# Infini-attention with a GEGLU gate: one broadcast tile for all head groups, the residual loaded once per segment, guard squares in halves

## The chip, the core and the metric

The kernel runs on one core of one Trainium2 chip. A core has five engines that run side by side, each with a queue of its own that is worked off in order: PE (matrix products; PEld is its loading of weights), DVE and POOL (elementwise work), ACT (functions by table), SP (here: it starts DMA transfers). DMAs are started by an instruction on an engine's queue and land later; engines wait for one another, and for DMAs, by semaphores. An instruction that waits holds up everything behind it in its queue. Times are device microseconds (us) of one execution; the figure given for a kernel is the median of its runs.

## What is computed

`x` has 2048 rows of 448; there are 16 heads of 28. The result is `x + attn * silu(gelu(xn wg) * (xn wu) wd)` with `xn` the layer norm of `x`.

```python
for s in range(4):                       # segments of 512 rows
    p = softmax(qs @ ks^T * 28**-0.5, causal within the segment)
    a_dot = p @ vs
    a_mem = (phi(qs) @ M) / (phi(qs) @ z + 1e-6)     # phi(t) = t+1 if t>0 else exp(t)
    o = g * a_mem + (1 - g) * a_dot                  # g = sigmoid(beta), one per head
    M += phi(ks)^T @ vs ;  z += sum(phi(ks))
s = o @ wo
out = x + s * silu((gelu(xn @ w_gate) * (xn @ w_up)) @ w_down)
```

## The kernel before

All of it is in `fast_path`. The rows are taken in 4 segments `s` of 512, each as 4 blocks of 128. The heads are padded from 28 to 32 and lie in 4 groups of 4, so that a group fills 128 partitions; the spare columns of a head make the denominators.

The program's order is written by hand (L523 to L581): the layer norm and the projections of segment 0; then for each segment `gate_up(s)`, 14 steps of 8 products each (gate, then up, then GELU on ACT and a product on DVE into `hT`), and `attention(s)`, 24 slots (4 groups x 3 banks x 2 head pairs). `gate_up(3)` comes after `attention(3)`, and after it the down projection and the finish of each block. Between steps and slots stand other pieces, by a table of step numbers (`in_turn`) or, in attention, as fill by weight. `tick` counts steps, slots and fill units; `later(n, fn)` issues `fn` n ticks on.

One slot of attention: `scores` puts K^T Q of two heads on PE (L337), ACT takes the exponential into `pt` (L341), POOL sets the masked half of the diagonal block to zero (L344, one or two per slot). Two banks later `pv` multiplies by V on PE (L354) into the one `pv` buffer that there is, and after a group's last bank `evac` copies it out on DVE (L364) and sends the denominators, one row per head, to DRAM (`den`, L366). The last two banks of a segment (`ends`) are issued at the head of the next `gate_up` or attention.

The denominators: `invert` (L379) loads all 16x512 of a segment and side (softmax, or memory) spread on 128 partitions (`dc`, L383), and 3 ticks on DVE multiplies by the gate and inverts. Four DMAs on SP write four copies to DRAM (`rdr`, L390), and four more, one per group, read them back repeated 32 times per head (`rb`, one 128x512 tile per group, L393). POOL multiplies the memory result by its `rb` (`scale_memory`, L401), and the softmax result by its own, adding the two (`combine`, L410 and L411).

`finish_units`: for a block, SP loads 128 rows of `x` again (`xr`, L458), PE multiplies by `wo` (L461), DVE multiplies by the SiLU part (L464), POOL adds `xr` (`o_out`, L466), SP stores (L467). Blocks of segment s-1 are finished within attention s, those of segment 3 at the end.

`guard` squares the raw query and key weights on ACT (L157) at step 4 of `gate_up(0)` and sums them on PE at step 9, for a bound on the scores; the first tile that held the query weights is one of the two buffers `oT`.

SP's queue carries nearly all DMAs, in program order: `den`, `dc`, `rdr`, `rb`, `xr`, the stores. A store waits for POOL's `o_out`, and whatever stands behind it in the queue waits too.

Of the kernel before, what the change touches and what calls it, by code (L numbers as in the profile page):

```python
# [8 lines left out]
ACT = mybir.ActivationFunctionType  # L9
ALU = mybir.AluOpType  # L10
# [15 lines left out]
def fast_path(tc, A_x, A_wq, A_wk, A_wv, A_wo, A_beta, B_w_gate, B_w_up, B_w_down, out):  # L26
# [16 lines left out]
    with ExitStack() as ctx:  # L43
# [8 lines left out]
        oup = pool("oup", 4)  # L52
        rbp = pool("rbp", 4)
        blk = pool("blk", 5)
# [28 lines left out]
        wq_raw = seg2.tile([DC, NDC, D], BF16, name="oT")  # L83
        wk_raw = const.tile([DC, NDC, D], BF16, name="wk_raw")
        wv_sb = const.tile([DC, NDC, D], BF16, name="wv_sb")
# [55 lines left out]
        def later(n, fn):  # L141
            waiting.append((clock[0] + n, len(waiting), fn))

        def tick():
            clock[0] += 1
            due = sorted(w for w in waiting if w[0] <= clock[0])
            waiting[:] = [w for w in waiting if w[0] > clock[0]]
            for _, _, fn in due:
                fn()
# [3 lines left out]
        def guard():  # L153
            sqs = {}
            for i, nm in enumerate(("wq", "wk")):
                sqs[nm] = oup.tile([DC, NDC, D], BF16, name=f"oU{i}")
                nc.scalar.activation(out=sqs[nm][:], in_=raw[nm][:], func=ACT.Square)  # L157
            ones = const.tile([P, 1], BF16, name="ones")
            nc.gpsimd.memset(ones[:], 1.0)
            nrm = small.tile([1, 2, H], F32, name="nrm")  # L160
            yield
            for i, nm in enumerate(("wq", "wk")):
                np_ = ps_m.tile([P, L], F32, name="m")
                for c in range(NDC):
                    nc.tensor.matmul(out=np_[0:1, 0:D], lhsT=ones[0:DC, :], rhs=sqs[nm][:, c, :],
                                     start=(c == 0), stop=(c == NDC - 1))
                nc.vector.reduce_sum(out=nrm[:, i, :],
                                     in_=np_[0:1, 0:D].rearrange("p (h d) -> p h d", d=Dh), axis=AX.X)
            okh = small.tile([1, H], F32, name="okh")
            nc.vector.tensor_tensor(out=okh[:], in0=nrm[:, 0, :], in1=nrm[:, 1, :], op=ALU.mult)  # L170
            nc.vector.tensor_scalar(out=okh[:], in0=okh[:], scalar1=(LOGIT_MAX / (D * scale)) ** 2,
                                    scalar2=None, op0=ALU.is_lt)
            nc.vector.tensor_reduce(out=oki[:], in_=okh[:], op=ALU.min, axis=AX.X)
            yield
# [67 lines left out]
        def project_units(s):  # L242
# [37 lines left out]
            def ktok(b):  # L280
                kp = ps_m.tile([P, L], F32, name="m")
                for c in range(NDC):
                    nc.tensor.matmul(out=kp[:, 0:D], lhsT=xnT[s][:, c, b * P:(b + 1) * P],  # L283
                                     rhs=wk_raw[:, c, :], start=(c == 0), stop=(c == NDC - 1))
                e = work.tile([P, D], BF16, name="phk_e")
# [22 lines left out]
        def update(s):  # L308
# [10 lines left out]
            if s == 0:  # L319
                nc.vector.tensor_tensor(out=macc[:], in0=u[:], in1=bd, op=ALU.mult)  # L320
            else:
                um = rbp.tile([P, G, P], F32, name="rb")
                nc.vector.tensor_tensor(out=um[:], in0=u[:], in1=bd, op=ALU.mult)
                nc.gpsimd.tensor_tensor(out=macc[:], in0=macc[:], in1=um[:], op=ALU.add)
# [43 lines left out]
        def memory_read(s, g):  # L368
# [3 lines left out]
            if g == G - 1:  # L372
                later(2, lambda: invert(s, 1))
                for i in range(G):
                    later(11 + 2 * i, lambda i=i: scale_memory(s, i))

        rb = {}

        def invert(s, side):  # L379

            dc = small.tile([P, 64], F32, name="dc")
            rdr = dram.tile([H, 4, L], F32, name="rdr")
            nc.sync.dma_start(out=dc[:], in_=den[s][side].rearrange("h (c f) -> (h c) f", f=64))  # L383

            def rest():
                nc.vector.tensor_scalar(out=dc[:], in0=dc[:], scalar1=(1e-6 if side else 0.0),
                                        scalar2=igate[:, side:side + 1], op0=ALU.add, op1=ALU.mult)
                nc.vector.reciprocal(out=dc[:], in_=dc[:])
                for j in range(4):
                    nc.sync.dma_start(out=rdr[:, j, :].rearrange("h (c f) -> h c f", f=64), in_=dc[:])  # L390
                for g in range(G):
                    r = rbp.tile([P, L], F32, name="rb")
                    nc.sync.dma_start(  # L393
                        out=r[:], in_=rdr[g * HG:(g + 1) * HG].rearrange("h j l -> (h j) l")
                        .unsqueeze(1).to_broadcast([HG * 4, HP // 4, L]))
                    rb[s, g, side] = r
            later(3, rest)

        def scale_memory(s, g):
            o_n = oU[s, g, 1]  # L400
            nc.gpsimd.tensor_tensor(out=o_n[:], in0=o_n[:], in1=rb.pop((s, g, 1))[:], op=ALU.mult)  # L401

        def combine(s, g):
# [3 lines left out]
            if s == 0:  # L407
                nc.gpsimd.tensor_tensor(out=dst, in0=o_a[:], in1=r[:], op=ALU.mult)
            else:
                nc.gpsimd.tensor_tensor(out=o_a[:], in0=o_a[:], in1=r[:], op=ALU.mult)  # L410
                nc.gpsimd.tensor_tensor(out=dst, in0=o_a[:], in1=oU.pop((s, g, 1))[:], op=ALU.add)  # L411
# [19 lines left out]
        def down_units(s):  # L431
# [21 lines left out]
            return u  # L453

        def finish_units(s):
            def fin(b):
                xr = work.tile([P, D], BF16, name="xr")
                nc.sync.dma_start(out=xr[:], in_=x_v[s][:, b, :])  # L458
                a_ps = ps_m.tile([P, L], F32, name="m")
# [5 lines left out]
                o_out = work.tile([P, D], BF16, name="o_out")  # L465
                nc.gpsimd.tensor_tensor(out=o_out[:], in0=t[:], in1=xr[:], op=ALU.add)  # L466
                nc.sync.dma_start(out=o_v[s][:, b, :], in_=o_out[:])  # L467
            return [(0.75, lambda b=b: fin(b)) for b in range(NB)]
# [54 lines left out]
        with tc.manual_schedule():  # L523
# [4 lines left out]
            for s in range(NSEG):  # L528
                last = s == NSEG - 1

                if not last:
# [5 lines left out]
                    else:  # L537
                        in_turn(table, 4, [lambda: next(check)])
                        in_turn(table, 9, [lambda: next(check)])
                    layer_norm_steps(s + 1, table)  # L540
# [3 lines left out]
                if s + 2 < NSEG:  # L544
                    load_x(s + 2)
                if s == 2:
                    ok = nc.values_load(oki[0:1, 0:1], min_val=0, max_val=1)
                pre, lists, at = [], [], {}
                if last:
                    in_turn(at, 0, ends)  # L550
                    in_turn(at, 2, [lambda: invert(s - 1, 0)])
                    in_turn(at, 10, [lambda g=g: combine(s - 1, g) for g in range(G)])
                    in_turn(at, 15, [lambda g=g: memory_read(s, g) for g in range(G)])
                elif s > 0:
# [15 lines left out]

            s = NSEG - 1
            table = {}
            in_turn(table, 0, ends)
            in_turn(table, 2, [lambda: invert(s, 0)])
            in_turn(table, 9, [lambda g=g: combine(s, g) for g in range(G)])
            gate_up(s, table)
            dn, fi = down_units(s), finish_units(s)
            for b in range(NB):
                run(dn[3 * b:3 * b + 3])
                run(fi[b:b + 1])  # L580
        return ok  # L581

# [381 lines left out]
```

## Time and profile before

| | us |
|---|---|
| median of 3 runs (lowest to highest) | 333.48 (332.92 to 333.96) |
| the profiled execution | 333.42 |
| its span | 331.6 |
| PE busy in the span | 279.2 (84%) |
| DVE, ACT, POOL busy | 159.5, 152.0, 132.9 |
| mean granted PE clock, share of full speed | 0.951 |

The span is the time between the first and the last instruction in the trace; 1.8 us of the execution lie outside. A busy PE isn't PE at full speed: the clock that is granted stands beside it. Idle time of an engine that is not waited for costs nothing, so the waits of PE and what releases it count most, then the queue of the releaser.

### The profile page before, as it was taken

What the parts mean: (1) busy time and instruction counts of PE and PEld (TensorE: products, weight loads), DVE (VectorE), ACT (ScalarE), POOL (GpSimd) and SP (SyncE); (2) the same over time, 40 slices, a digit from 0 to 9 for tenths busy, and PEclk for the clock granted to TensorE, in tenths of its full rate; (3) what the DMA queues carried; (4) which work ended last, traced back from release to release, by engine and by line L of the source; (5) the groups of instructions that cost most, each with busy time, mean ns of one, the idle gap of its engine ahead of it and who ended that gap; (6) DMA issues with size and microseconds to landing.
All of it is one profiled execution on the core that took longest, in us unless ns stands there. A gap on an engine that the chain in (4) does not pass through costs nothing.

```text
span 331.6 us, 4480 instructions
## 1 busy us (share of the span) xinstructions
PE 279.2 (84%) x1620; PEld 116.1 (35%) x1620; DVE 159.5 (48%) x301; ACT 152.0 (46%) x213; POOL 132.9 (40%) x219
## 2 busy tenths in 40 slices
PE   0699989999999999989999998198837973979691
PEld 0344434433334434333444432022312321434250
DVE  2447746645559567655585576145202531233221
ACT  1324542867772355556733386246643650223010
POOL 7000100333311245459410983286546743216712
PEclk9999999999999999999999999659996997799898
DMA  6998000000000520340102300510050021514011
GB/s 199 267 265 211 0 1 2 0 2 4 0 3 5 144 56 21 85 102 29 33 6 70 74 8 18 155 43 29 22 135 9 8 59 57 143 22 140 0 55 51
DMA packets 20773, 21.00 MB, mean 63 GB/s; under 512 B 6424, under 2 KB 16152, under 8 KB 20744
## 3 DMA queue, kind: packets, MB, share of 16 engines
q1 hardware_dynamic: 19512, 18.41, 21.3%
q10 hardware_dynamic: 1200, 2.24, 2.5%
q8 instruction: 14, 0.23, 0.3%
q14 instruction: 15, 0.12, 0.1%
q0 software_dynamic: 32, 0.00, 0.0%
HBM read 17.66 MB, written 2.98 MB: 62 GB/s over the span
## 4 chain that ended last, share of the span: by engine, by line
PE 54%; DMA 16%; POOL 11%; SPq 6%; DVE 5%; ACT 3%; issue 3%; POOLq 0%; DVEq 0%; ACTq 0%
PE s L422 21%; PE m L253 8%; PE m L437 7%; DMA xr<-in_A_x_dram 6%; PE s L337 5%; PE m L275 3%; DMA rdr<-dc 3%; POOL o_out L466 3%; POOL oU L410 3%; PE pv L354 3%; POOL oT L411 3%; PE m L283 3%; SPq L390 2%; SPq L393 2%; DMA oT<-in_A_wq_dram 2%
## 5 line engine op out<-in xcount | busy, mean ns | idle before, releaser
L341 ACT ACTIVATE pt<-s 128x1024 bf16<-128x1024 f32 (+1 forms) x96 | 81.6, 883 | 45.3 <-PE s L337 33.7
L344 POOL TENSOR_SCALAR_AFFINE_SELECT pt<-pt 128x256 bf16<-128x256 bf16 x128 | 51.7, 424 | 66.8 <-ACT pt L341 63.8
L425 ACT ACTIVATE gl<-s 128x512 bf16<-128x512 f32 x56 | 33.3, 597 | 75.1 <-PE s L422 75.0
L422 PE MATMUL s<-xnT,wg_sb 112*128 112x512 bf16 x224 | 58.9, 386 | 3.3 <-DVE hT L426 3.3
L426 DVE TENSOR_TENSOR hT<-gl,s 128x512 bf16<-128x512 bf16 x56 | 38.1, 683 | 49.2 <-ACT gl L425 49.1
L422 PE MATMUL s<-xnT,wu_sb 112*128 112x512 bf16 x224 | 58.4, 384 | 0.0
L437 PE MATMUL m<-wd_sb,hT 128*128 128x448 bf16 x224 | 51.8, 368 | 0.0
L354 PE MATMUL pv<-pt,vaug 128*32 128x512 bf16 (+3 forms) x256 | 21.2, 324 | 24.6 <-POOL pt L344 17.0
L337 PE MATMUL s<-qT,kT 32*128 32x128 bf16 (+3 forms) x256 | 33.1, 309 | 2.5 <-ACT pt L341 2.3
L466 POOL TENSOR_TENSOR o_out<-sg,xr 128x448 bf16<-128x448 f32 x16 | 16.9, 1059 | 41.0 <-DMA xr<-in_A_x_dram 31.4
L422 PEld LDWEIGHTS <-wu_sb 112*128 112x128 bf16 x224 | 22.1, 99 | 27.1 <-issue 1.3
L422 PEld LDWEIGHTS <-wg_sb 112*128 112x128 bf16 x224 | 21.1, 99 | 27.6 <-issue 6.4
L437 PEld LDWEIGHTS <-hT 128*128 128x128 bf16 x224 | 20.4, 101 | 22.6 <-issue 6.8
L194 POOL TENSOR_TENSOR rstd<-rstd,nhalf 128x2 f32<-128x2 f32 x8 | 5.8, 727 | 48.2 <-DVE rstd L192 48.1
L364 DVE COPY oU<-pv 128x512 f32<-128x512 f32 x16 | 11.0, 686 | 25.5 <-PE pv L354 15.3
L410 POOL TENSOR_TENSOR oU<-oU,rb 128x512 f32<-128x512 f32 x12 | 15.2, 1266 | 19.6 <-DMA rb<-rdr 19.6
L337 PEld LDWEIGHTS <-kT 32*128 32x128 bf16 x256 | 9.9, 92 | 37.2 <-issue 36.5
L446 DVE SCALAR_TENSOR_TENSOR sg<-th,m 128x448 f32<-128x448 f32 x16 | 9.9, 619 | 26.6 <-ACT th L441 24.4
L253 PE MATMUL m<-xnT,wq_pad 112*128 112x512 bf16 x64 | 19.1, 427 | 0.7 <-ACT xnT L209 0.7
L354 PEld LDWEIGHTS <-vaug 128*32 128x32 bf16 x256 | 6.5, 94 | 37.4 <-issue 34.2
L253 PE MATMUL m<-xnT,wk_pad 112*128 112x512 bf16 x64 | 18.6, 418 | 0.0
L461 PE MATMUL m<-wo_sb,oT 128*128 128x448 bf16 x64 | 16.0, 369 | 3.0 <-POOL oT L411 3.0
(76 smaller groups left out, 275.3 us busy)
## 6 DMA issues: line engine op xcount, KB each, us to landing
rb<-rdr SPq DMA_DIRECT2D x28, 256.0 KB
xr<-in_A_x_dram SPq DMA_DIRECT2D x16, 112.0 KB
out_dram<-o_out SPq DMA_DIRECT2D x16, 112.0 KB
x_sb<-in_A_x_dram SPq DMA_DIRECT2D x7, 224.0 KB
wu_sb<-in_B_w_up_dram ACTq DMA_DIRECT2D x1, 1568.0 KB
wg_sb<-in_B_w_gate_dram SPq DMA_DIRECT2D x1, 1568.0 KB
wd_sb<-in_B_w_down_dram SPq DMA_DIRECT2D x1, 1568.0 KB
rdr<-dc SPq DMA_DIRECT2D x28, 32.0 KB
```

The lines of the kernel that those rows point to most:

```text
L253: nc.tensor.matmul(out=pr[:], lhsT=wpad[nm][:, c, g * HG:(g + 1) * HG, :].rearrange("p h d -> p (h d)"), rhs=xnT[s][:, c, :], start=(c == ...
L337: nc.tensor.matmul(out=sp[:, j, c0:c0 + n], lhsT=kT[s][r, g, kb * P:(kb + 1) * P], rhs=qT[s][r, g, kb * P:L], start=True, stop=True)
L341: nc.scalar.activation(out=pt[:, :, 0:w], in_=sp[:, :, 0:w], func=ACT.Exp, scale=scale)
L344: nc.gpsimd.affine_select(out=v, in_=v, pattern=[[0, 2], [1, P]], compare_op=ALU.is_ge, fill=0.0, base=0, channel_multiplier=-1)
L354: nc.tensor.matmul(out=acc[i * HP:(i + 1) * HP, kb * P:L], lhsT=va[:, kb, g * HG + i, :], rhs=pts[i // 2][:, i % 2, c0:c0 + n], start=(kb ...
L410: nc.gpsimd.tensor_tensor(out=o_a[:], in0=o_a[:], in1=r[:], op=ALU.mult)
L422: nc.tensor.matmul(out=gu[:, i, :], lhsT=w_sb[:, c, fc * P:(fc + 1) * P], rhs=xnT[s][:, c, :], start=(c == 0), stop=(c == NDC - 1))
L425: nc.scalar.activation(out=gl[:], in_=gu[:, 0, :], func=ACT.Gelu_apprx_tanh)
L426: nc.vector.tensor_tensor(out=hT[s][:, fc, :], in0=gl[:], in1=gu[:, 1, :], op=ALU.mult)
L437: nc.tensor.matmul(out=d_ps[:, 0:D], lhsT=hT[s][:, fc, b * P:(b + 1) * P], rhs=wd_sb[:, fc, :], start=(fc == 0), stop=(fc == NFC - 1))
L461: nc.tensor.matmul(out=a_ps[:, 0:D], lhsT=oT[s][:, g, b * P:(b + 1) * P], rhs=wo_sb[:, g, :], start=(g == 0), stop=(g == G - 1))
L466: nc.gpsimd.tensor_tensor(out=o_out[:], in0=t[:], in1=xr[:], op=ALU.add)
```

## The change

`rb` becomes one tile [128, 4, 512] for all groups, of which there is one buffer. `rdr` holds one copy. The four broadcast DMAs are one per head slot i, each writing partitions 32i to 32i+31 for all four groups. Every `scale_memory` and `combine` thus reads what all four DMAs wrote, and the next broadcast waits until all readers of the last are done. `xr` is loaded once per segment, [128, 4, 448], on ACT's queue, ahead of the attention that finishes the segment, for segment 3 ahead of the last `gate_up`; it has one buffer. The add and the store of a block come one tick later. The squares are issued in four halves, one per step from step 4, and their check at step 8. The raw key weights lie in the other `oT` buffer, so the keys in row form (`ktok`, L283) are made from the padded weights, with 28 of every 32 columns read. The scaling of the memory result is due at ticks 9 to 12 after the memory read in place of 11, 13, 15, 17; three table entries move by one.

```diff
-        rbp = pool("rbp", 4)
+        rbp = pool("rbp", 1)
-        wk_raw = const.tile([DC, NDC, D], BF16, name="wk_raw")
+        wk_raw = seg2.tile([DC, NDC, D], BF16, name="oT")
...
-                nc.scalar.activation(out=sqs[nm][:], in_=raw[nm][:], func=ACT.Square)
+                for c in range(0, NDC, 2):
+                    nc.scalar.activation(out=sqs[nm][:, c:c + 2, :], in_=raw[nm][:, c:c + 2, :],
+                                         func=ACT.Square)
+                    yield
...
-                                     rhs=wk_raw[:, c, :], start=(c == 0), stop=(c == NDC - 1))
+                                     rhs=wpad["wk"][:, c, :, 0:Dh], start=(c == 0), stop=(c == NDC - 1))
...
-                    later(11 + 2 * i, lambda i=i: scale_memory(s, i))
+                    later(9 + i, lambda i=i: scale_memory(s, i))
...
-            rdr = dram.tile([H, 4, L], F32, name="rdr")
+            rdr = dram.tile([H, L], F32, name="rdr")
-                for j in range(4):
-                    nc.sync.dma_start(out=rdr[:, j, :].rearrange("h (c f) -> h c f", f=64), in_=dc[:])
+                nc.sync.dma_start(out=rdr[:].rearrange("h (c f) -> (h c) f", f=64), in_=dc[:])
+                r = rbp.tile([P, G, L], F32, name="rb")
+                rdr_v = rdr[:].rearrange("(g i) l -> i g l", i=HG)
+                for i in range(HG):
+                    nc.sync.dma_start(out=r[i * HP:(i + 1) * HP, :, :],
+                                      in_=rdr_v[i].unsqueeze(0).to_broadcast([HP, G, L]))
                 for g in range(G):
-                    r = rbp.tile([P, L], F32, name="rb")
-                    nc.sync.dma_start(
-                        out=r[:], in_=rdr[g * HG:(g + 1) * HG].rearrange("h j l -> (h j) l")
-                        .unsqueeze(1).to_broadcast([HG * 4, HP // 4, L]))
-                    rb[s, g, side] = r
+                    rb[s, g, side] = r[:, g, :]
...
+        def reload_x(s):
+            xr[s] = seg1.tile([P, NB, D], BF16, name="xr")
+            nc.scalar.dma_start(out=xr[s][:], in_=x_v[s])
+
         def finish_units(s):
             def fin(b):
-                xr = work.tile([P, D], BF16, name="xr")
-                nc.sync.dma_start(out=xr[:], in_=x_v[s][:, b, :])
...
-                nc.gpsimd.tensor_tensor(out=o_out[:], in0=t[:], in1=xr[:], op=ALU.add)
-                nc.sync.dma_start(out=o_v[s][:, b, :], in_=o_out[:])
+                def rest():
+                    nc.gpsimd.tensor_tensor(out=o_out[:], in0=t[:], in1=xr[s][:, b, :], op=ALU.add)
+                    nc.sync.dma_start(out=o_v[s][:, b, :], in_=o_out[:])
+                later(1, rest)
...
+                if s > 0:
+                    reload_x(s - 1)
...
             s = NSEG - 1
+            reload_x(s)
             table = {}
             in_turn(table, 0, ends)
-            in_turn(table, 2, [lambda: invert(s, 0)])
-            in_turn(table, 9, [lambda g=g: combine(s, g) for g in range(G)])
+            in_turn(table, 3, [lambda: invert(s, 0)])
+            in_turn(table, 10, [lambda g=g: combine(s, g) for g in range(G)])
```

The first place is SP's queue at the end of attention(3) and the start of the last `gate_up`, before the change:

```order
L366 DMA den<-oU_2855 4x512
L458 DMA xr<-in_A_x_dram 128x448
L467 DMA out_dram<-o_out 128x448
L383 DMA dc<-den 128x64
L366 DMA den<-oU_2891 4x512
L458 DMA xr<-in_A_x_dram 128x448
L467 DMA out_dram<-o_out 128x448
L458 DMA xr<-in_A_x_dram 128x448
L467 DMA out_dram<-o_out 128x448
L458 DMA xr<-in_A_x_dram 128x448
L467 DMA out_dram<-o_out 128x448
L390 DMA rdr<-dc 16x8x64 x4
```

and after it, where the same lines have other numbers (L368 `den`, L385 `dc`, L391 `rdr`, L395 `rb`, L475 the store):

```order
L368 DMA den<-oU_2795 4x512
L385 DMA dc<-den 128x64
L475 DMA out_dram<-o_out 128x448
L368 DMA den<-oU_2851 4x512
L475 DMA out_dram<-o_out 128x448
L391 DMA rdr<-dc 128x64
L395 DMA rb<-rdr 32x4x512 x4
L475 DMA out_dram<-o_out 128x448 x2
L368 DMA den<-oU_2954 4x512
L385 DMA dc<-den 128x64
```

No load of `xr` stands between the stores any more, and the write and broadcast of the inverse come ahead of the last two stores.

The second place is POOL in attention(2), where the blocks of segment 1 are finished and the memory result of segment 2 is scaled, before:

```order
L344 AFFINE_SELECT pt<-pt 128x2x128 x6
L466 TENSOR_TENSOR o_out<-sg,xr 128x448
L344 AFFINE_SELECT pt<-pt 128x2x128 x4
L466 TENSOR_TENSOR o_out<-sg,xr 128x448
L401 TENSOR_TENSOR oU_2116<-oU_2116,rb 128x512
L344 AFFINE_SELECT pt<-pt 128x2x128 x4
L401 TENSOR_TENSOR oU_2133<-oU_2133,rb 128x512
```

and after (L346 is the select, L474 the add, L403 the scaling):

```order
L346 AFFINE_SELECT pt<-pt 128x2x128 x6
L474 TENSOR_TENSOR o_out<-sg,xr 128x448
L346 AFFINE_SELECT pt<-pt 128x2x128 x2
L403 TENSOR_TENSOR oU_2096<-oU_2096,rb 128x512
L346 AFFINE_SELECT pt<-pt 128x2x128
L403 TENSOR_TENSOR oU_2113<-oU_2113,rb 128x512
L346 AFFINE_SELECT pt<-pt 128x2x128
L403 TENSOR_TENSOR oU_2118<-oU_2118,rb 128x512
```

The first scaling has moved two selects and one add ahead.

The third place is ACT before the last `gate_up`, before:

```order
L341 ACTIVATE pt<-s 128x1024 x4
L341 ACTIVATE pt<-s 128x2x256 x2
L425 ACT_TABLE_LOAD
L425 ACTIVATE gl<-s 128x512 x14
L441 ACTIVATE th<-m 128x448 x4
```

and after (L343 is the exponential, L427 the GELU, L443 the tanh):

```order
L343 ACTIVATE pt<-s 128x1024 x4
L343 ACTIVATE pt<-s 128x2x256 x2
L461 DMA xr<-in_A_x_dram 128x4x448
L427 ACT_TABLE_LOAD
L427 ACTIVATE gl<-s 128x512 x14
L443 ACTIVATE th<-m 128x448 x4
```

The load of `xr` for segment 3 now stands ahead of the function table of GELU; it goes into the one `xr` buffer, so it waits for POOL's last `o_out` of segment 2.

## Rows read from the trace of the kernel before

**Rows 1.** PE's waits by line in four stretches in order: us, times, longest us.
```profile
PE pv L354 <- POOL pt L344: 0.9, 1, 0.9
...
PE pv L354 <- POOL pt L344: 7.5, 2, 6.7
...
PE pv L354 <- DVE oU L364: 7.0, 1, 7.0
PE pv L354 <- POOL pt L344: 1.5, 3, 0.7
...
PE pv L354 <- POOL pt L344: 7.1, 4, 4.0
```
**Rows 2.** Timeline in gate_up(0): start, us, engine, line, what, [idle before <-releaser].
```profile
43.44 1.02 PE L422 MATMUL s<-xnT,wg_sb 112*128 112x512 bf16 x4 [1.39 <-DVE hT L426]
```
**Rows 3.** Groups by line and shape: count | busy us, mean ns | idle before.
```profile
L157 ACT ACTIVATE oU<-oT 112x1792 bf16<-112x1792 bf16 x1 | 1.7, 1689 | 0.0
L466 POOL TENSOR_TENSOR o_out<-sg,xr 128x448 bf16<-128x448 f32 x16 | 16.9, 1059 | 41.0 <-DMA xr<-in_A_x_dram 31.4 <-DVE sg L464 9.6
L283 PE MATMUL m<-wk_raw,xnT 112*128 112x448 bf16 x48 | 10.6, 354 | 0.1
```
**Rows 4.** Timeline in attention(2).
```profile
206.28 2.48 SPq L393 DMA_DIRECT2D rb<-rdr  x4
...
209.39 0.44 SPq L458 DMA_DIRECT2D xr<-in_A_x_dram  x1
213.13 1.03 POOL L466 TENSOR_TENSOR o_out<-sg,xr 128x448 bf16<-128x448 f32 x1 [9.59 <-DMA xr<-in_A_x_dram]
...
214.57 0.76 PE L354 MATMUL pv<-pt,vaug 128*32 128x256 bf16 x4 [6.72 <-POOL pt L344]
```
**Rows 5.** Stretches: us, busy PE, PEld, DVE, ACT, POOL, granted PE clock, DMA, GB/s.
```profile
210.00:220.00 10.00, 5.43 (x22) 1.42 (x21) 1.84 (x3) 1.02 (x1) 5.71 (x10) 0.51 0.34 87
220.00:230.00 10.00, 8.62 (x54) 2.69 (x51) 6.29 (x10) 6.54 (x9) 8.88 (x14) 0.81 0.07 21
```
**Rows 6.** Timeline in attention(3).
```profile
239.57 2.50 SPq L390 DMA_DIRECT2D rdr<-dc  x4
...
243.49 2.48 SPq L393 DMA_DIRECT2D rb<-rdr  x4
...
250.44 0.62 PE L354 MATMUL pv<-pt,vaug 128*32 128x512 bf16 x4 [7.03 <-DVE oU L364]
```
**Rows 7.** DMA traffic between 244.5 and 249 us.
```profile
DMA packets 563, 1.04 MB, mean 232 GB/s; under 512 B 54, under 2 KB 54, under 8 KB 563
```
**Rows 8.** Timeline at the start of the last gate_up.
```profile
268.03 0.39 PE L354 MATMUL pv<-pt,vaug 128*32 128x512 bf16 x2 [0.90 <-POOL pt L344]
...
269.43 1.04 PE L422 MATMUL s<-xnT,wg_sb 112*128 112x512 bf16 x4
...
270.21 1.28 ACT L425 ACT_TABLE_LOAD   x1
...
280.53 0.40 PE L354 MATMUL pv<-pt,vaug 128*32 128x256 bf16 x2 [3.96 <-POOL pt L344]
...
286.49 1.03 PE L422 MATMUL s<-xnT,wg_sb 112*128 112x512 bf16 x4
...
288.21 1.03 PE L422 MATMUL s<-xnT,wg_sb 112*128 112x512 bf16 x4
...
293.79 1.02 PE L422 MATMUL s<-xnT,wg_sb 112*128 112x512 bf16 x4 [1.96 <-DVE hT L426]
```
**Rows 9.** Timeline of the tail.
```profile
300.87 1.27 POOL L410 TENSOR_TENSOR oU<-oU,rb 128x512 f32<-128x512 f32 x1 [9.29 <-DMA rb<-rdr]
...
312.45 0.46 PE L461 MATMUL m<-wo_sb,oT 128*128 128x448 bf16 x1 [2.19 <-POOL oT L411]
...
325.37 0.62 DVE L464 TENSOR_TENSOR sg<-sg,m 128x448 f32<-128x448 f32 x1
326.62 1.03 POOL L466 TENSOR_TENSOR o_out<-sg,xr 128x448 bf16<-128x448 f32 x1 [2.69 <-DMA xr<-in_A_x_dram]
```

More of the change, by code (lines that the diff above doesn't have):

```diff
@@ L141, in later @@
         def later(n, fn):
-            waiting.append((clock[0] + n, len(waiting), fn))
+            waiting.append((clock[0] + n, clock[0], fn))
         def tick():
             clock[0] += 1
-            due = sorted(w for w in waiting if w[0] <= clock[0])
+            due = sorted((w for w in waiting if w[0] <= clock[0]), key=lambda w: w[:2])
             waiting[:] = [w for w in waiting if w[0] > clock[0]]
@@ L160, in guard @@
             nrm = small.tile([1, 2, H], F32, name="nrm")
-            yield
             for i, nm in enumerate(("wq", "wk")):
@@ L321, in update @@
             else:
-                um = rbp.tile([P, G, P], F32, name="rb")
+                um = rbp.tile([P, G, P], F32, name="um")
                 nc.vector.tensor_tensor(out=um[:], in0=u[:], in1=bd, op=ALU.mult)
@@ L400, in scale_memory @@
             o_n = oU[s, g, 1]
-            nc.gpsimd.tensor_tensor(out=o_n[:], in0=o_n[:], in1=rb.pop((s, g, 1))[:], op=ALU.mult)
+            nc.gpsimd.tensor_tensor(out=o_n[:], in0=o_n[:], in1=rb.pop((s, g, 1)), op=ALU.mult)
         def combine(s, g):
@@ L407, in combine @@
             if s == 0:
-                nc.gpsimd.tensor_tensor(out=dst, in0=o_a[:], in1=r[:], op=ALU.mult)
+                nc.gpsimd.tensor_tensor(out=dst, in0=o_a[:], in1=r, op=ALU.mult)
             else:
-                nc.gpsimd.tensor_tensor(out=o_a[:], in0=o_a[:], in1=r[:], op=ALU.mult)
+                nc.gpsimd.tensor_tensor(out=o_a[:], in0=o_a[:], in1=r, op=ALU.mult)
                 nc.gpsimd.tensor_tensor(out=dst, in0=o_a[:], in1=oU.pop((s, g, 1))[:], op=ALU.add)
@@ L453, in down_units @@
             return u
+        xr = {}
+        def reload_x(s):
+            xr[s] = seg1.tile([P, NB, D], BF16, name="xr")
+            nc.scalar.dma_start(out=xr[s][:], in_=x_v[s])
         def finish_units(s):
             def fin(b):
-                xr = work.tile([P, D], BF16, name="xr")
-                nc.sync.dma_start(out=xr[:], in_=x_v[s][:, b, :])
                 a_ps = ps_m.tile([P, L], F32, name="m")
@@ L537, in fast_path @@
                     else:
-                        in_turn(table, 4, [lambda: next(check)])
-                        in_turn(table, 9, [lambda: next(check)])
+                        in_turn(table, 4, [lambda: next(check)] * 5)
                     layer_norm_steps(s + 1, table)
@@ L552, in fast_path @@
                     in_turn(at, 10, [lambda g=g: combine(s - 1, g) for g in range(G)])
-                    in_turn(at, 15, [lambda g=g: memory_read(s, g) for g in range(G)])
+                    in_turn(at, 14, [lambda g=g: memory_read(s, g) for g in range(G)])
                 elif s > 0:
@@ L580, in fast_path @@
                 run(fi[b:b + 1])
+            tick()
         return ok
```

## Prediction, on record before the changed kernel was run

> **What bounds the kernel now.** I read the table first: PE is busy 84% of the span, at a mean clock of 0.951, so what a change can win are PE's gaps and the stretches at a lower clock. Then PE's waits by line, in the stretches 120 to 189, 189 to 232 (attention(2)), 232 to 268 (attention(3)) and 267 to the end [rows 1]: nearly all are `pv` behind POOL's select, except one of 7.0 behind the copy of `pv`. Then who makes POOL late. Over its 16 adds `o_out`, POOL stood 31.4 us for `xr` [rows 3]; attention(2) shows how [rows 4]: `xr` is asked for at 209.39 on SP, behind four broadcasts issued from 206.28, the add waits 9.59 and starts at 213.13, the select stands behind it on POOL, and PE stands 6.72. After such a stop PE runs at a lower clock: 0.51 over 210 to 220, 0.81 over 220 to 230 [rows 5], where full speed is 1.00 (2.4 GHz) and half of it 1.2 GHz. So the bound around the change is the chain SP's queue, DMA, POOL, PE.
>
> **The change part by part**, against the profiled execution of 333.42 (span 331.6 and 1.8 outside; the median of the runs is 333.48, so nothing has to be shifted).
>
> A, squares. Two of 1.69 us [rows 3] stand on ACT between the GELUs of neighbouring steps, and PE then waits 1.39 for `hT` [rows 2]. A half takes about 0.85, beside a GELU it fits in a step of 1.72 (288.21 less 286.49) [rows 8]. -1.4; at worst two halves of it come back as waits, -0.7.
>
> B, attention(1): one wait of 0.9 of the same kind [rows 1]; `xr` now lands long before. -0.9.
>
> C, attention(2). At most the 7.5 of PE's waits [rows 1] and what the clock cost: 5.43 busy at 0.51 is 2.8 at full speed, 8.62 at 0.81 is 7.0, so 2.6 and 1.6, 4.2 in all [rows 5]; together 11.7. Not all of it goes. The add no longer waits, and next on POOL, after two selects, is the first scaling, which now needs all four broadcasts. These were issued from 206.28; three writes of `rdr` fewer ahead of them, 2.50 for four [rows 6], so 1.9, put that at 204.4. A broadcast of all four took 5.4 from first issue to last byte (243.49 to 248.9, the 1.04 MB of [rows 7]), so it is there at 209.8. POOL stood at the add from 213.13 less 9.59, 203.5; with an add of 1.06 and two selects it reaches the scaling at 205.5 or later and waits up to 4.3. Of the 9.59 PE felt 6.72, so 2.9 was slack; 1.4 is left for PE, and I add half of the clock's loss, 2.1: 3.5 stays. -8.2, bounds -10.3 (no wait, a little of the clock's loss) and -4 (each of four scalings holds a select back).
>
> D, attention(3). The 1.5 of `pv` behind the select [rows 1] has its 0.7 behind an add waiting for `xr`: -0.7. Of four such waits in the next stretch, 7.1 in all [rows 1], the first, 0.90 at 268.03, lies before the last `gate_up` [rows 8]: -0.9. (The other three, 6.2, are in E.) The 7.03 before a `pv` at 250.44 [rows 6] is another matter: POOL combines as the broadcasts land, and the select, the memory read's copy and `pv` queue behind. It gets three writes less, -1.9, but now the first combine waits for the last of four DMAs, not the first: data ran 3.9 us for the four, so the first was whole some 3.5 after issue and the last at 5.4, +1.9. I take 0, with -1.9 (the order of bytes doesn't matter) and +4 (the full 3.9 of data is added) as bounds.
>
> E, start of the last `gate_up`. From 269.43 to 286.49 PE does four steps and the last `pv` products, in 17.06 [rows 8]. Four steps need 4 x 1.72. The twelve `pv` products take 0.76 for four at the low clock [rows 4], so 2.3 for all and half of it, 1.2, at the full one; I take 1.3, together 8.2. The rest is the three waits, and half clock after the longest. All three were behind adds waiting for `xr`, and stores and loads of it took turns on SP; now neither is there. -8.9. What is late next: ACT's GELU now stands behind the load of `xr`, which waits for the last add of segment 2 (after DVE's 0.62 and an add of 1.06), then the table load of 1.28 [rows 8], a GELU and `hT`, against a PE that may run two steps and the `pv` products ahead, 3.4 + 1.3. These nearly cancel; I take 0, with 2.0 against it at worst.
>
> F. PE's 1.96 at 293.79 [rows 8] was `hT` on DVE behind `dc`, whose denominators stood on SP behind the four writes and four broadcasts of the other side. With three writes less and the queue some us earlier, -2.0; bounds -2.0 and 0.
>
> G, tail. The combine waits for `rb` 9.29 at 300.87, and PE 2.19 for its result [rows 9]. The chain (write, broadcast 5.4, four combines) starts earlier with the steps, one step later by the table, and ends after PE needs it as before: 0, bounds -2.2 and +2.
>
> H. The last add waits for `xr` 0.6 beyond DVE's end (325.37 + 0.62 to 326.62) [rows 9]: -0.6.
>
> I. Added: four issues on ACT, some 0.5 each by SP's 0.44 [rows 4], beside PE's work mostly; and the 48 products of `ktok`, 0.354 each [rows 3], now stream 28 of 32 columns. No row shows a strided moving operand: bounds 0 and, at twice the time, 48 x 0.215 (the full clock's pace of a step's 8 products, 1.72 / 8, 512 columns), 10.3. I take +1.0 for both, nearer to the lower end, since the products move as many columns as before.
>
> Sum: -1.4 - 0.9 - 8.2 - 0.7 - 0.9 - 8.9 - 2.0 - 0.6 + 1.0 = -22.6. The time is 333.42 - 22.6 = 310.8.
>
> **A rule against it.** The rows: four broadcasts of 128 partitions moved 1.04 MB at 232 GB/s on the mean of 4.5 us, 3.9 us of traffic [rows 7]. The Trainium skill, SBUF — State Buffer, section "Door 1: The DMA port swizzle", says that a transfer reaches only the ports of its partitions, 32 neighbours half of the sixteen, with 218 in place of 436 GB/s as the limit. Its section "Can I just issue two DMAs to hit both halves?" doubts that transfers to different partitions add up. By its figure my estimate would be 4.8 us a broadcast, not 3.9, and 2.7 more over three places on the path. The trace of before holds no broadcast of 32 partitions, so it doesn't show which holds.
>
> **The rivals.**
> 1. The broadcast per head runs at half the pace, 7.8 for 3.9 us, since each of its DMAs writes a quarter of the partitions. It is on the path in C, D and G: +11.7, 322.5. For it: nothing that was measured; against it: four DMAs together still fill all partitions, and moved bytes are the same.
> 2. POOL is the jam in attention(2): each scaling waits and three of them are now one select apart, so C gives 4 and the clock stays low: +4.2, 315.0. For it: the select stands behind whatever POOL does [rows 4].
> 3. Slower than before: the 32 readers of one copy collide. Before, four copies were each read eight times; now one is read 32 times. At a quarter of the pace a broadcast takes 15.6, 11.7 more at three places, 35.1: 345.9. It decides from 22.6 / 3 = 7.5 more per broadcast on, 11.4 us for 1 MB. For it: four copies are written where one would do, at 0.63 each on SP; against it: no row shows a collision.
> 4. The strided products take twice the time: +10.3 less the 1.0 taken, some 9.3, 320.1.
> 5. The stalls in D and G go too, since SP's queue is emptier: -4.1 and up to 3 of C's remainder, 303.7.
>
> **How the numbers follow.** Forecast 0.58, rival 1 0.11, rival 2 0.12, rival 3 0.05, rival 4 0.05, rival 5 0.09. The forecast's own range, from its smaller unknowns, is 305 to 316. The whole range is 302.5 to 322.5: it holds rivals 1 (its near half), 2, 4 and 5 and leaves out some 0.15. A measurement of this kernel can tell about 0.3%, 1 us, from no change. Faster by more: all but rival 3 and a remainder of mishaps, 0.93; within it 0.02; slower 0.05.
>
> **What would show it.** C, E: no waits of POOL for `xr`, no stretch at 0.51, PE's `pv` waits under 2 us in attention(2), four steps in about 8.5 at the start of the last `gate_up`. A: no 1.39 at fc 4 or 5. D: a wait near 7 before a `pv` in attention(3). F: no 1.96. G: some 3 us of PE at the tail behind the combine. Rivals 1 and 3: the traffic of a broadcast lasts 7.8 or 15.6 us. Rival 4: `ktok`'s products near 0.7. I would be wrong by most if POOL's wait for `rb`, or ACT's for the last add, simply takes the place of the wait for `xr`.

## The result, and the profile after

The changed kernel took 323.61 us (318.33 to 324.15 over four timed executions) against 333.24 before; the comparison's ratio is 0.962, interval 0.950 to 0.975. It is faster, by 10 to 15 us and not by the 22.6 that the sum gave. Its executions fall into two groups, 318.3 once and 323 to 324 otherwise, of which the ratio counts 318.33 and 323.08 alone; the profile below is the one of 318.33 (span 316.6), and the second trace, further on, shows where the other 5 us lie. Of the range that was put on record, 302.5 to 322.5, the execution of 318.33 lies inside and the median 1.1 above the upper end.

Stage by stage, by PE's products in the traces (us; a `gate_up` runs from its first product to the start of its last four, an attention from there to the first product of the next `gate_up`, attention(3) begins with its first score, and the tail ends with the span):

| | before | changed | xr alone on ACT | changed, less two parts | with a fifth buffer |
|---|---|---|---|---|---|
| to gate_up(0) | 29.58 | 28.87 | 29.56 | 28.65 | 29.81 |
| gate_up(0) | 27.47 | 25.95 | 27.48 | 25.95 | 25.96 |
| attention(1) | 43.51 | 43.73 | 42.37 | 42.37 | 42.37 |
| attention(2) | 42.35 | 38.03 | 32.23 | 33.33 | 32.77 |
| attention(3) | 38.84 | 37.67 | 36.97 | 36.57 | 34.13 |
| gate_up(3) | 35.58 | 26.31 | 30.29 | 25.91 | 25.54 |
| tail | 26.59 | 28.36 | 23.92 | 26.53 | 26.64 |

Stages that are left out are equal to 0.1. Some expectations below end attention(2) one slot earlier, at 39.95 before and 35.97 or 35.98 after the change; with the boundary of the table these are 42.35 and 38.03. The last three columns are experiments (the fourth is the changed kernel without the new broadcast and the early scaling, the fifth builds on it). The third already says much: one part of the change alone does better than the whole.

What the change was to remove, it removed. Of the groups by line and shape, the row of the adds [rows 3] has become

```profile
L474 POOL TENSOR_TENSOR o_out<-sg,xr 128x448 bf16<-128x448 f32 x16 | 17.0, 1062 | 12.5 <-DVE sg L470 10.1 <-issue 2.4
L285 PE MATMUL m<-wk_pad,xnT 112*128 112x448 bf16 x48 | 10.6, 354 | 0.1
```

No wait for `xr` is left of 31.4 us, and the strided `ktok` takes its old 354 ns.

In attention(2), though, another wait stands at the same place. The timeline there (start, us, engine, line, what, idle before and releaser), beside [rows 4]:

```profile
200.98 1.74 SPq L395 DMA_DIRECT2D rb<-rdr  x4
...
201.93 1.03 POOL L474 TENSOR_TENSOR o_out<-sg,xr 128x448 bf16<-128x448 f32 x1
...
208.75 1.26 POOL L403 TENSOR_TENSOR oU<-oU,rb 128x512 f32<-128x512 f32 x1 [4.99 <-DMA rb<-rdr]
...
209.97 0.41 POOL L346 TENSOR_SCALAR_AFFINE_SELECT pt<-pt 128x256 bf16<-128x256 bf16 x1
...
210.34 1.30 POOL L403 TENSOR_TENSOR oU<-oU,rb 128x512 f32<-128x512 f32 x1
210.42 0.39 PE L356 MATMUL pv<-pt,vaug 128*32 128x512 bf16 x2 [1.45 <-POOL pt L346]
...
212.42 1.26 POOL L403 TENSOR_TENSOR oU<-oU,rb 128x512 f32<-128x512 f32 x1
212.50 0.61 PE L356 MATMUL pv<-pt,vaug 128*32 128x512 bf16 x2 [1.69 <-POOL pt L346]
```

POOL now waits 4.99 at the first scaling, 7.77 us after the first of the four broadcasts was issued, and then each select comes behind a scaling of 1.26, with PE behind the select. PE's waits by line (us, times, longest) are, in attention(2) and then from its last two slots to the last `gate_up` (the 8.6 is in attention(3)),

```profile
PE pv L356 <- POOL pt L346: 4.2, 3, 1.7
...
PE pv L356 <- DVE oU L366: 9.0, 2, 8.6
```

against 7.5 and 7.0 before [rows 1]. The stop in attention(3) [rows 6] has grown from 7.03 to 8.55, and its chain can be read upward from PE:

```profile
233.51 1.74 SPq L395 DMA_DIRECT2D rb<-rdr  x4
...
241.08 1.26 POOL L412 TENSOR_TENSOR oU<-oU,rb 128x512 f32<-128x512 f32 x1 [3.43 <-DMA rb<-rdr]
...
243.71 0.69 DVE L366 COPY oU<-pv 128x512 f32<-128x512 f32 x1 [11.68 <-POOL oT L413]
...
244.46 0.62 PE L356 MATMUL pv<-pt,vaug 128*32 128x512 bf16 x4 [8.55 <-DVE oU L366]
```

PE waits for a copy on DVE, the copy for POOL's combine, the combine for `rb`, and `rb` is read 7.57 after the first issue at 233.51. The old form of broadcast reaches its first reader in 3.30 (a row of it stands with the experiments).

At the start of the last `gate_up`, four steps with the `pv` products take 9.5 us and no longer 17.06; what is late there is ACT, held by its load of `xr`, and PE behind it:

```profile
264.92 0.38 ACTq L461 DMA_DIRECT2D xr<-in_A_x_dram  x1
...
265.33 1.28 ACT L427 ACT_TABLE_LOAD   x1 [2.63 <-POOL pt L346]
...
267.99 1.02 PE L424 MATMUL s<-xnT,wg_sb 112*128 112x512 bf16 x4 [1.77 <-DVE hT L428]
```

### The profile page after: what moved, and what is told of

Same layout as the page of the kernel before. It is cut to its first block, busy times and chain, and to the rows that moved or that the text cites. A ratio compares the mean times of both kernels' runs of the same rounds, so it can differ in the third digit from the quotient of the medians.

```text
span 316.6 us, 4442 instructions
## 1 busy us (share of the span) xinstructions
PE 273.9 (87%) x1619; PEld 114.6 (36%) x1620; DVE 160.8 (51%) x301; ACT 152.7 (48%) x215; POOL 132.5 (42%) x219
## 5 line engine op out<-in xcount | busy, mean ns | idle before, releaser
L343 ACT ACTIVATE pt<-s 128x1024 bf16<-128x1024 f32 (+1 forms) x96 | 82.0, 883 | 38.9 <-PE s L339 37.1
L346 POOL TENSOR_SCALAR_AFFINE_SELECT pt<-pt 128x256 bf16<-128x256 bf16 x128 | 51.6, 421 | 69.1 <-ACT pt L343 68.8
L427 ACT ACTIVATE gl<-s 128x512 bf16<-128x512 f32 x56 | 33.3, 597 | 61.4 <-PE s L424 61.3
L424 PE MATMUL s<-xnT,wg_sb 112*128 112x512 bf16 x224 | 57.6, 379 | 2.0 <-DVE hT L428 2.0
L424 PE MATMUL s<-xnT,wu_sb 112*128 112x512 bf16 x224 | 57.5, 379 | 0.0
L439 PE MATMUL m<-wd_sb,hT 128*128 128x448 bf16 x224 | 52.5, 372 | 0.2 <-issue 0.2
L356 PE MATMUL pv<-pt,vaug 128*32 128x512 bf16 (+3 forms) x256 | 19.9, 317 | 14.7 <-DVE oU L366 9.5
L412 POOL TENSOR_TENSOR oU<-oU,rb 128x512 f32<-128x512 f32 x12 | 15.2, 1264 | 22.0 <-DMA rb<-rdr 22.0
L474 POOL TENSOR_TENSOR o_out<-sg,xr 128x448 bf16<-128x448 f32 x16 | 17.0, 1062 | 12.5 <-DVE sg L470 10.1
L403 POOL TENSOR_TENSOR oU<-oU,rb 128x512 f32<-128x512 f32 x12 | 15.1, 1266 | 15.5 <-DMA rb<-rdr 15.5
L262 DVE CAST kT<-m 128x512 bf16<-128x512 f32 x16 | 11.0, 689 | 15.4 <-PE m L255 15.3
L443 ACT ACTIVATE th<-m 128x448 f32<-128x448 f32 x16 | 8.7, 544 | 20.5 <-PE m L439 20.4
L255 PE MATMUL m<-xnT,wq_pad 112*128 112x512 bf16 x64 | 17.9, 406 | 0.7 <-ACT xnT L211 0.7
```

Source lines behind the costliest of these rows:

```text
L255: nc.tensor.matmul(out=pr[:], lhsT=wpad[nm][:, c, g * HG:(g + 1) * HG, :].rearrange("p h d -> p (h d)"), rhs=xnT[s][:, c, :], start=(c == ...
L343: nc.scalar.activation(out=pt[:, :, 0:w], in_=sp[:, :, 0:w], func=ACT.Exp, scale=scale)
L346: nc.gpsimd.affine_select(out=v, in_=v, pattern=[[0, 2], [1, P]], compare_op=ALU.is_ge, fill=0.0, base=0, channel_multiplier=-1)
L356: nc.tensor.matmul(out=acc[i * HP:(i + 1) * HP, kb * P:L], lhsT=va[:, kb, g * HG + i, :], rhs=pts[i // 2][:, i % 2, c0:c0 + n], start=(kb ...
L412: nc.gpsimd.tensor_tensor(out=o_a[:], in0=o_a[:], in1=r, op=ALU.mult)
L424: nc.tensor.matmul(out=gu[:, i, :], lhsT=w_sb[:, c, fc * P:(fc + 1) * P], rhs=xnT[s][:, c, :], start=(c == 0), stop=(c == NDC - 1))
```

## The experiments

The theory after this result: the whole gain is `xr` off SP's queue, with the squares; the new broadcast and the early scaling each give part of it back. The rivals stand with each run. All ratios are to runs of the kernel before on the same chip.

**xr alone** (kernel before, plus only this):

```diff
-                xr = work.tile([P, D], BF16, name="xr")
-                nc.sync.dma_start(out=xr[:], in_=x_v[s][:, b, :])
+            xr[s] = seg1.tile([P, NB, D], BF16, name="xr")     # reload_x, on ACT's queue
+            nc.scalar.dma_start(out=xr[s][:], in_=x_v[s])
```

> The kernel before with one part of the change alone: xr once per segment on ACT's queue. Theory 1 (the gain is SP's queue: the adds no longer wait for xr behind broadcasts and stores): no POOL wait for xr; attention(2) 5 to 8 us shorter than the 39.95 of before, the last gate_up some 7 us shorter than 35.58 (its 1.96 stays), gate_up(0) unchanged with its 1.39; in all 315 to 319. Rival (the gain is the broadcast: three writes fewer and the inverse ahead of the stores): 328 or more.

313.5 us, ratio 0.938 (0.933 to 0.944). It beats the whole change, and the expected 315 to 319. Attention(2) is 10.1 shorter than before, more than the 5 to 8 expected, the last `gate_up` 5.3 where some 7 were expected, and no wait in attention(2) is for POOL:

```profile
PE s L337 <- ACT pt L341: 2.7, 5, 0.7
PE pv L354 <- DVE oU L364: 1.4, 2, 0.9
```

PE's clock is 1.00 throughout that stage. The rival falls.

**Old broadcast in the changed kernel.** Four copies and one DMA per group again, in the form of the kernel before:

```diff
-                    nc.sync.dma_start(out=r[i * HP:(i + 1) * HP, :, :],
-                                      in_=rdr_v[i].unsqueeze(0).to_broadcast([HP, G, L]))
+                    nc.sync.dma_start(out=r[:], in_=rdr[g * HG:(g + 1) * HG].rearrange("h j l -> (h j) l")
+                                      .unsqueeze(1).to_broadcast([HG * 4, HP // 4, L]))
```

> The changed kernel with the old broadcast: four copies in DRAM, one DMA of 128 partitions per group, one tile per group. Theory 1 (the broadcast per head slot is a loss inside the change: 7.6 us from the first issue to the first POOL reader, against 3.6 to 5.4 before): first reader 3.6 to 4.5 us after the first issue, the stop before pv in attention(3) about 7 and not 8.6, PE's waits for the combine at the tail under 4.5; 3 to 6 us faster than the changed kernel. Rival (the three extra writes at 0.63 us each and their landing cost as much): within 1 us of it.

316.77, ratio 0.946 (0.943 to 0.950). Attention(3) fell from 37.67 to 36.05, its stop from 8.6 to 6.8, as expected, but attention(2) rose from 38.03 to 40.44: 4.5 us of PE's waits for the select, where the changed kernel has 4.2, and then a clock of 0.50 for the rest of the stage. In all it is 1.6 faster than the execution of 318.33 and 6.8 faster than the median.

**Old ticks of the scaling in the changed kernel:**

```diff
-                    later(9 + i, lambda i=i: scale_memory(s, i))
+                    later(11 + 2 * i, lambda i=i: scale_memory(s, i))
```

> The changed kernel with the scaling of the memory result at ticks 11, 13, 15, 17 after the memory read as before. Theory 1 (in attention(2) each early scaling holds a select back, 4.2 us of PE's waits): these waits shrink to 1 or 2 us and attention(2) is 2 to 3 us shorter than 35.97. Rival (POOL is late anyway by its sum of work): attention(2) within 0.5 us of 35.97.

317.50, ratio 0.951 (0.947 to 0.954). The waits for the select fell from 4.2 to 1.2 as expected, but attention(2) only from 38.03 to 36.82, where 2 to 3 us were expected: from 213 to its end the clock is 0.50. Attention(1) lost its 1.36 as well.

**Both** edits, the changed kernel less two parts:

> The changed kernel with both the old broadcast (four copies, one DMA per group) and the old ticks 11, 13, 15, 17 of the scaling. Theory 1 (these two parts are what the change loses against xr on ACT alone): 310 to 313, attention(2) near 32.2, attention(3) near 36 to 37. Rival (something else in the change loses: the add one tick later, the last inversion one step later, the strided ktok): still 316 or more.

309.32, ratio 0.927 (0.921 to 0.933). With this the four corners are: old broadcast and old ticks 309.3, new broadcast alone 317.5, early scaling alone 316.8, both 323.6. Each part costs some 6 to 8 us by itself (8.2 and 7.5 by the medians, 7.7 and 6.3 by the ratios), and together 14 by the median, 9 by the execution of 318.33. The clock is in these prices: its mean in attention(2) is 1.00 with neither part, 0.86 with the new broadcast alone and 0.84 with the early scaling alone. The rival, that something else in the change loses, falls; what is left of the change over `xr` alone gains another 4: 1.5 by the squares, and 4.4 in the last `gate_up`, of which the tail gives 2.6 and attention(2) 1.1 back; which edit does the latter no run separates.

**Early scaling with `xr` alone**, the same test from the other side (`later(9 + i` in the kernel with only `xr` on ACT).

> The kernel before with xr once per segment on ACT, and the scaling of the memory result at ticks 9 to 12 in place of 11 to 17; nothing else. Theory 1 (an early scaling waits for rb on POOL and each one holds a select back): PE waits for POOL's select 3 to 5 us in attention(2), where xr on ACT alone has none; attention(2) 34 to 40 (40 where the PE clock falls after the waits) and not 32.23. Rival (the early scaling is harmless with the old broadcast): within 1 us of 32.23.

318.26, ratio 0.956 (0.951 to 0.961), 4.8 slower than without; attention(2) takes 40.07. Waits of PE in attention(2), and stretches of it (us, busy PE, PEld, DVE, ACT, POOL, granted clock, DMA, GB/s):

```profile
PE pv L354 <- POOL pt L344: 4.4, 4, 1.6
```

```profile
210.00:215.00 5.00, 2.13 (x12) 0.78 (x12) 1.89 (x3) 2.47 (x4) 5.00 (x7) 1.00 0.17 47
215.00:220.00 5.00, 3.83 (x15) 1.09 (x15) 0.69 (x1) 0.72 (x1) 3.55 (x7) 0.61 0.07 23
220.00:225.00 5.00, 5.00 (x26) 1.24 (x25) 2.90 (x5) 3.29 (x5) 1.91 (x6) 0.50 0.00 0
```

POOL is busy all the time from 210 to 215, PE 2.13 of 5; behind that PE runs full at half the clock. So the old broadcast doesn't save the early scaling: POOL reaches it before `rb` is there, then scalings and selects alternate.

**The changed kernel again**, for a second trace.

> The changed kernel, unaltered, for a second trace of it: its executions took 318.3 once and 323.1 to 324.2 four times. Theory: the 5 us are TensorE's clock behind the waits of attention(2); an execution near 323.5 shows attention(2) at 40 to 41 us with stretches at 0.50 as in the kernel with the old broadcast and early scaling, where the first trace has 35.98 with one stretch at 0.66; all other stages within 0.6 us of the first trace. Rival: the 5 us lie in another stage (the stop in attention(3), the tail).

324.37. Attention(2) takes 41.23, and PE's waits for the select in it are the same, 4.1 in three. What differs is the clock; these are stretches of the first and then of the second trace:

```profile
211.23:216.23 5.00, 3.51 (x12) 0.85 (x12) 1.57 (x2) 1.14 (x2) 5.00 (x7) 0.66 0.07 23
216.23:221.23 5.00, 4.18 (x31) 1.54 (x31) 1.38 (x2) 2.08 (x4) 3.59 (x8) 1.00 0.07 25
```

```profile
211.23:216.23 5.00, 3.51 (x12) 0.84 (x12) 1.57 (x2) 1.15 (x2) 5.00 (x7) 0.57 0.07 23
216.23:221.23 5.00, 4.20 (x15) 1.18 (x15) 0.69 (x1) 1.50 (x2) 3.19 (x7) 0.50 0.07 25
221.23:226.23 5.00, 5.00 (x26) 1.28 (x25) 2.90 (x5) 3.02 (x4) 2.28 (x6) 0.50 0.01 2
```

In 4.2 us of busy time PE does 31 products in the one and 15 in the other. Attention(2) gave 3.2 of the 5.9 us of span, less than I expected; the rest is 0.7 in attention(3), 1.3 in `gate_up(3)` and 0.7 in the tail. The mean clock is lower in `gate_up(3)` (0.94 for 1.00), hardly in attention(3) (0.85 for 0.86) and not in the tail (0.86 for 0.85), so what made these two longer stays open. Why the clock differs after equal waits no run shows.

**Why the new broadcast is slow.** Three runs.

> The changed kernel with one copy in DRAM, but one DMA of 128 partitions per group into a tile of its own. If the slow traffic comes from DMAs that write only 32 partitions: 1 MB takes about 3.9 us again, the first group is whole some 3.6 us after the first issue, and this is faster than with four copies by up to 2 us (three writes fewer). If it comes from 32 readers of one copy: 1 MB takes 5.3 us or more as in the changed kernel.

> The changed kernel with the broadcast still one DMA of 32 partitions per head slot, but from four copies in DRAM, each read by 8 partitions and not 32 (denominators and gates reordered to head slot by group, so that a slot's four rows are contiguous). If the 32 readers of one copy make the traffic slow: 1 MB takes about 3.9 us again. If the 32 partitions do: 5.3 us or more as in the changed kernel. The time: within 3 us of 318 to 323 either way, since three writes at 0.63 us come back on SP.

> The changed kernel, but the four broadcast DMAs per head slot read 1 MB of constants in DRAM in which each of the 32 partitions has rows of its own (written once, early); the inverse denominators are not used, so the attention part of the output is another. Same instructions, same partitions, same 2 KB pieces; only the sharing of rows is gone. If 32 readers of one row make the broadcast slow: 1 MB in about 3.9 us, first reader some 6 us after the first issue. If 32 partitions per DMA do: 5.3 us of traffic or more and 7.5 us to the first reader, as in the changed kernel.

The edits, in the changed kernel (own rows: `rows` holds 1 MB of ones, written once):

```diff
+ group1:   out=r[:],  in_=rdr[g * HG:(g + 1) * HG].unsqueeze(1).to_broadcast([HG, HP, L])
+ head4:    out=r[i * HP:(i + 1) * HP],  in_=rdr[i].rearrange("j g l -> j (g l)").unsqueeze(1).to_broadcast([4, HP // 4, G * L])
+ own rows: out=r[i * HP:(i + 1) * HP],  in_=rows[i].rearrange("g p l -> p g l")
```

Stretches within a broadcast, of the changed kernel, then of the one less two parts (old broadcast), own rows, one copy per group, and four copies per head slot (columns as above):

```profile
235.50:239.00 3.50, 0.40 (x3) 0.19 (x3) 0.00 (x0) 1.45 (x3) 1.56 (x5) 1.00 1.03 236
```

```profile
232.00:235.00 3.00, 0.00 (x0) 0.00 (x0) 0.00 (x0) 0.00 (x0) 1.36 (x2) 0.59 0.99 277
```

```profile
281.50:285.00 3.50, 3.50 (x18) 1.57 (x16) 1.38 (x2) 1.19 (x2) 0.00 (x0) 1.00 1.02 252
```

```profile
286.00:288.00 2.00, 2.00 (x9) 0.83 (x8) 0.65 (x1) 0.21 (x1) 0.44 (x1) 0.84 0.26 102
```

```profile
274.00:278.00 4.00, 0.00 (x0) 0.00 (x0) 0.00 (x0) 0.00 (x0) 0.00 (x0) 0.50 0.26 107
```

The last two failed as tests of the readers. Both took 0.26 of the DMA engines and some 105 GB/s, whatever the copies: their DMAs have 4 as the first count of the source, the fast forms 16 or 32. The one with four copies per head slot took 373.48 (ratio 1.121, 1.116 to 1.125), far from the 318 to 323 that I expected; one copy per group 317.57 (0.950, 0.946 to 0.955). The Trainium skill, DMA: Bandwidth & Descriptors, section "Why a DMA increments its semaphore by 16 and not by 1", says that the number of engines is the largest, up to 16, that divides the slowest dimension of both sides; 0.26 for a count of 4 agrees.

Own rows settles the readers, with the same 32 partitions and nothing shared. Over its seven broadcasts the first reader comes 6.7 to 7.7 us after the first issue (median 7.0), in the changed kernel 7.4 to 9.9 (median 7.5), so sharing a row is worth some 0.5 us. Here is the last broadcast of own rows, with 7.65, and then one of the old form, with 3.30:

```profile
279.16 2.84 SPq L403 DMA_DIRECT2D rb<-rows  x4
...
286.81 1.26 POOL L420 TENSOR_TENSOR oU<-oU,rb 128x512 f32<-128x512 f32 x1 [12.27 <-DMA rb<-rows]
```

```profile
230.40 2.48 SPq L395 DMA_DIRECT2D rb<-rdr  x4
...
233.70 1.26 POOL L412 TENSOR_TENSOR oU<-oU,rb 128x512 f32<-128x512 f32 x1 [1.60 <-DMA rb<-rdr]
```

So it isn't, in the main, the readers of one copy. Its time was 319.15 in one run. Part is the pace (236 and 252 GB/s against 277, and in the changed kernel a first and a last microsecond at some half of that, 5.4 us of traffic in all against some 4.3): in attention(3) the last packet ends 6.6 us after the first issue in the changed kernel and 5.7 in the old form. That is 0.9 of the 4.3 us by which the first reader comes later there; the larger part is that it waits for all four DMAs, where the old form's reader started on the first. This split is read from the traces; no run separates the two in the kernel's time. The Trainium skill, SBUF — State Buffer, "Can I just issue two DMAs to hit both halves?", has two transfers into different halves at only 6% more than one. With the 218 GB/s that the prediction took for one, that would be 231, an estimate from that page's figures; the 236 and 252 lie above it, but they are read in the middle of a transfer, and 1 MB in 5.4 us is some 194, so these runs don't decide.

**Better versions.** First `xr` alone with the squares in halves, and the load for segment 3 moved into step 1 of the last `gate_up`; then the changed kernel less two parts with that load moved; then a fifth buffer for the softmax result on top.

```diff
             table = {}
-            reload_x(s)
+            in_turn(table, 1, [lambda: reload_x(s)])
```

> The kernel before with three edits: xr once per segment on ACT, the guard squares in four halves, and the load of xr for segment 3 issued in step 1 of the last gate_up, behind the function table of GELU. Theory 1: gate_up(0) 25.95 in place of 27.48, the 1.83 that PE waits for hT early in the last gate_up gone; against xr on ACT alone 2 to 3.3 us faster, 309 to 312. Rival (the wait only moves, the tail gives it back): within 1.5 us, the squares alone.

313.4, ratio 0.940 (0.936 to 0.944): no gain over `xr` alone, less even than the squares' 1.5. The wait moved: later in the stage PE stood 5.5 us for `hT`, behind `dc` on DVE.

> The changed kernel with the old broadcast and the old ticks of the scaling, and the load of xr for segment 3 in step 1 of the last gate_up. Theory: the 1.77 that PE waits for hT early in the last gate_up goes, since ACT no longer waits for the last add of segment 2 before GELU's table: 307 to 309 where the kernel without this edit took 309.3. Rival (the step before the combine at the tail only waits longer): within 0.5 us of 309.3.

309.6, ratio 0.927 (0.919 to 0.935): the time is the rival's. The early wait of 1.77 is gone, but 10 us further on PE now waits for `hT` behind `dc` on DVE, as it did in the kernel before [rows 8], and the tail is 0.5 longer:

```profile
269.36 0.26 DVE L388 TENSOR_SCALAR dc<-dc,igate 128x64 f32<-128x64 f32 x1 [2.00 <-DMA dc<-den]
...
270.80 1.02 PE L424 MATMUL s<-xnT,wg_sb 112*128 112x512 bf16 x4 [1.35 <-DVE hT L428]
```

> As best3, and a fifth buffer for the softmax result. Theory: the stop of 6.7 to 8.6 us before pv in attention(3) is DVE's copy of pv that waits for a free buffer, which POOL's first combine releases; with a fifth buffer the copy goes at once and the stop falls below 2 us: attention(3) 29 to 32 and not 36.6, in all 300 to 304. Rival (POOL's selects stand behind the combines, so pv waits for them all the same): within 2 us of best3.

```diff
+        oup0 = pool("oup0", 5)
-            t = oup.tile([P, L], F32, name=f"oU{side}")
+            t = (oup if side else oup0).tile([P, L], F32, name=f"oU{side}")
```

(In this run the guard's squares both lie in tiles named `oU1`; `gate_up(0)` stays at 25.96.)

306.51, ratio 0.918 (0.910 to 0.927), the fastest of the study, but 3 better and not 6 to 9, between theory and rival. The one stop of 6.6 is gone, and the waits of PE from 180 on are now

```profile
PE pv L357 <- POOL pt L347: 4.4, 5, 2.4
...
PE pv L357 <- DVE oU L367: 1.1, 2, 0.6
```

The buffer was the cause of the long stop, and the rival names what comes in its place: the selects stand behind the combines on POOL. Attention(3) is 34.13, 2.3 shorter than the 36.41 without the buffer and not the 29 to 32 expected.

## Why the prediction was right or wrong

The direction was right, and so was the source of the gain: POOL's waits for `xr` are gone. The working was wrong in what takes the place of the removed waits, nearly all of it behind the new broadcast and the early scaling. The sum came out 7.5 to 12.8 us too good (310.8 for 318.33 to 323.61), outside its own range of 305 to 316 in every execution.

A is right: 1.52 for 1.4. B is wrong as a sum: `xr` alone gave 1.14 in attention(1), the new scaling and the new broadcast together took it back (43.73; 42.52 with the old broadcast, 42.37 with the old ticks).

C is the step that failed: 4.3 (1.1 in the second trace) for 8.2. `xr` alone takes 10.1 out of this stage, where I put 11.7 as the most, and 5.8 of it comes back in place of my 3.5: PE waits 4.2 for the select where I had 1.4, and is busy 2.4 longer than with `xr` alone, at the lower clock, where I had 2.1 (its other waits are 0.8 shorter).

The failure is in "so it is there at 209.8" and in "1.4 is left for PE". POOL's wait for `rb` came out near, 4.99 for 4.3, by two errors against each other. The broadcast was issued 3.4 earlier than I put it (2.0 by the stages ahead), and it took 7.77 from the first issue to the reader and not 5.4: 6.75 to the last byte, on DMAs of another form, and 1.0 from there to the reader, which my sum did not have. (Even in the broadcast that I measured, the last packets end at 5.8; the window of [rows 7] closes ahead of them.)

And I let POOL wait once, where four scalings and the selects alternate: rival 2, at 0.12, is what the traces show, and in the second trace a clock of 0.50 behind it. Its 315.0 was still too good, since the tail and attention(3) lose to the late broadcast as well. I gave the late broadcast and the jam on POOL as alternatives; they are one chain. Rival 1's mechanism, half the pace, is not there: the traffic of 1 MB lasts 5.2 to 5.8 us in six of the seven broadcasts and not 7.8 (7.9 in the one beside the load of `xr` at 264.92, which is not in C, D or G). That its 322.5 lies near the median is chance.

D came out near, 1.2 for 1.6, by two errors against each other: without the new broadcast it gives 2.3 to 2.8, so the removal of `xr` from this stage was undervalued, and the later `rb` cost 1.1 to 1.6 where I took 0; the stop itself grew by 1.5. That cost was inside its bounds (-1.9 to +4).

E and F together gave 9.3 for 10.9. The missing 1.6 is the ACT wait that I named and took as hidden; PE's wait of 1.77 for `hT` is there, inside the bound of 2.0. Moving the load won 0.3 of it in the stage (25.60 for 25.91) and nothing in the time, since a wait behind `dc` like F's then came instead.

G and H: +1.8 for -0.6. PE waits 4.5 for the combine, not 3.0, and is busy 0.5 longer at the lower clock of the tail (0.85 against 0.90). G's bound of +2 held it.

I: nothing was added, against the 1.0; the strided products take 354 ns as before, so rival 4 falls. The rule that spoke against the change made its cost 2.7 in all; the two-by-two gives 8.2 for the broadcast, the clock included, and pace, which is what that rule is about, is the smaller part of the time to the reader. Rival 3 is excluded by the run with rows of its own.

The stages cover the whole difference: 22.6 forecast, 15.0 of span measured; C lacks 3.9, G and H 2.4, E and F 1.6, B 1.1, D 0.4, A, I and the start give 1.8 back.

## What to carry to other kernels

When a wait is removed from an engine that several streams share, list what comes next in that engine's queue and when its own data is there; here POOL's next wait, 4.99 us, was half as long as the 9.59 removed, and the work behind it on POOL then held PE three times. A broadcast whose pieces serve all consumers makes the first consumer wait for the last piece, so count to the reader and not to the last byte, and from a transfer of the same form. Changes that come in one package should be priced apart: one of these parts alone was faster than all of them together.

## What the runs showed of the hardware that I had not expected

Equal waits of PE led to different clocks: with 4.2 and 4.1 us of waits for the select in attention(2), the microseconds from 216 to 221 ran at 1.00 in one trace of the changed kernel and at 0.50 in the other, worth 3.2 us in that stage. From the last packet of a broadcast in the changed kernel to the first instruction that reads it some 1.0 us passed (6.75 to 7.77 after the first issue in attention(2)). And a DMA whose first count is 4 used 0.26 of the DMA engines at about 105 GB/s, whether its data was read 8 or 32 times.
